# Two units through each TensorE array mode together: regrouping the stages of a chunked retention and mixture-of-adapters kernel

## The chip, the cores and the metric

The kernel runs on one core of a Trainium2 chip. The time is device microseconds of one execution. The kernel before takes 194.24 us (median of three runs, 193.79 to 195.04). The profiled execution has a span of 191.0 us, and TensorE was granted 0.993 of its full clock over it.

## The reference

Two layers are computed, one after the other. For 8 sequences and 8 heads, with 576 positions and a head size of 64, the first is retention: attention without a softmax, with a decay that differs by head.

```python
scores = scale * np.matmul(q, k.transpose(0, 1, 3, 2))
gamma = 1.0 - 2.0 ** (-5.0 - np.arange(H, dtype=np.float32))
Dmat = np.where(rel >= 0, gamma[:, None, None] ** rel[None, :, :], 0.0)
ret = scores * Dmat[None, :, :, :]
return np.matmul(ret, v)
```

Its result, read as 4608 tokens of 512 values, goes through a mixture of 8 adapters of rank 16. For each token the two experts with the largest of the 8 logits `x @ w_gate` are taken, their logits pass a softmax over the two, and the output is `x` plus the weighted sum of `(x @ A[e]) @ B[e]`. Everything is in fp32 at the borders; the kernel keeps the second, small adapter product in fp16.

## The kernel before, in words

**Tiling.** The 576 positions are cut into four full chunks of 128 and a last one of 64. Sequences are taken in quads of four: one quad of one chunk is loaded by three DMAs (q, k and v). A full quad has two *units* of two sequences each; in the last chunk a unit takes four sequences of 64 positions. So units 0 to 15 are full (two units to a quad, two quads to a chunk) and units 16 and 17 make up the last chunk. A state `P` per unit position carries the decayed sum of k-times-v from chunk to chunk, which keeps the work linear in the number of chunks.

**Stages of a unit.** Each is a function that emits its instructions.

- T (line 268): TensorE transposes q and k, 16 matmuls each, into two PSUM banks each; ScalarE or VectorE copies them out (`qT`, `kT`).
- S (326): scores, in two halves of 16 matmuls, one per sequence. Each half fills two whole PSUM banks (`ps`), and VectorE multiplies each by the decay mask on its way to SBUF (`rt`).
- Q (304): the part of the output that comes from `P`, into the two banks `px`. U (374): the new state (`pu`, then `pn` on VectorE and `P` on GpSimd). R (402): scores times v, added into `px`; VectorE scales each bank out into `xT`.
- Z (484): adapter-down product and gate logits together (`pz`), then four kinds of small VectorE instructions on the logits. V (511): two sigmoids on ScalarE. W (524): VectorE picks the two experts and weights the adapter values (`zc`).
- B (449): transposes `xT` back to token rows, into the two banks `po`, which stay held. X (469): transposes `zc` (`pzt`, copied to `zT` by ScalarE). Y (549): adapter-up product added into `po`; four copies of a half bank take the result to `osb`, and DMAs write it.

**Array modes.** By the rows and columns of the array that its matmuls use, each stage is of one of four kinds: T, S and B use 64 rows by 128 columns (the profile's `64*128`), Q uses `64*64`, U and R `128*64`, and X, Z and Y `128*128`. In the last chunk S, Q and R are all `64*64`.

**Order.** The order is written out by hand. The helper `chain` (line 73) ties every instruction of TensorE, VectorE and ScalarE to the one emitted before it on the same engine, so that each engine runs exactly in the order in which the code calls the stages. Semaphores are added where data or buffers require them. In the steady loop (lines 673 to 694) one unit passes S, T of the next unit, B of the unit before, Q, U, R, and then X, Z and Y.

**PSUM.** The kernel hands out the eight banks itself, oldest free one first:

```python
def bank(shape, name, dtype=FP32):
    n = free.pop(0)
    x = pp.tile(shape, dtype, tag=f"bank{n}", name=name)
```

`done` puts a bank at the end of the list when the stage that reads it has been emitted. The next tile on that bank then waits, at its first matmul, until the reader of the old one has finished. So what counts is how many other banks are handed out in between.

**Other buffers.** q, k and v have three buffers each, so the load for the quad after next is issued at a quad's start. GpSimd scales k in place after its transpose (`scale_k`, line 255).

Of the kernel before, what the change touches and what calls it, by code (L numbers as in the profile page):

```python
# [10 lines left out]
FP32 = mybir.dt.float32  # L11
# [7 lines left out]
def kernel(  # L19
# [232 lines left out]
    def is_full(t):  # L252
        return units[t][0] < NFULL

    def scale_k(t):

        if not is_full(t):
            return
        kk = nat[units[t]][1]
        for b in range(2):  # L260
            gp.tensor_tensor(  # L261
                out=kk[:, b],
                in0=kk[:, b],
                in1=gv[:, 0].unsqueeze(2).broadcast_to((128, H, Dh)),
                op=ALU.mult,
            )

    def stage_T(t, names=("qT", "kT")):

        s = st.setdefault(t, {})  # L270
        for nm in names:
            src = nat[units[t]][0 if nm == "qT" else 1]
            dst = s[nm] = wk.tile([128, 2, HP, C], FP32, tag=nm, name=nm)
            ps = [bank([128, HP, 2, L], f"p{nm}") for _ in range(2)]
            for hp in range(HP):
                for b in range(2):
                    for g in range(2):
                        mm(
                            ps[g][:, hp, b, :],
                            lhsT=src[rows(g), b, 2 * hp : 2 * hp + 2, :],  # L280
                            rhs=id64[rows(g), :],
                            is_transpose=True,
                            start=True,
                            stop=True,
                        )
            for g in range(2):
                if is_full(t):
                    o = dst[:, :, :, rows(g)].rearrange("p b a i -> p a b i")
                else:
                    o = dst[:, g].rearrange("p a (b i) -> p a b i", b=2)  # L290
                if t == 0 and nm == "kT":
                    for b in range(2):
                        x = dst[:, b, :, rows(g)]
                        if g == 1:
                            vec("tensor_copy", out=x, in_=ps[g][:, :, b])
                        else:
                            act("copy", out=x, in_=ps[g][:, :, b])
                elif t < 2 and nm == "qT" or t < 3 and nm == "kT" and g == 1:
                    vec("tensor_copy", out=o, in_=ps[g])
                else:  # L300
                    act("copy", out=o, in_=ps[g])
            done(*ps)
# [99 lines left out]
    def stage_R(t):  # L402
        c, qd, sl = units[t]
        s = st[t]
        px, rt = s["px"], s["rt"]
        v32 = nat[units[t]][2]
        s["xT"] = []
        if is_full(t):
            for b in range(2):
                for hp in range(HP):  # L410
                    for ho in range(2):
                        h = 2 * hp + ho
                        mm(
                            px[b][rows(ho ^ b), hp, :],
                            lhsT=v32[:, b, h, :],
                            rhs=rt[(b, ho)][:, hp, :],
                            start=(c == 0 and hp == 0),
                            stop=True,
                            skip_group_check=True,
                        )  # L420
                xt = mo.tile([128, HP, C], FP32, tag="xT", name="xT", bufs=6)
                vec("tensor_tensor", out=xt, in0=px[b], in1=asc[b], op=ALU.mult)
                s["xT"].append(xt)
            done(*px)
            return
        for hp in range(HP):
            for y in range(2):
                for ho in range(2):
                    for x in range(2):
                        mm(  # L430
                            px[x][rows(ho ^ x), hp, rows(y)],
                            lhsT=v32[rows(x), y, 2 * hp + ho, :],
                            rhs=rt[ho][rows(x), hp, y, :],
                            start=False,
                            stop=True,
                            skip_group_check=True,
                        )
        for x in range(2):
            xt = mo.tile([128, HP, C], FP32, tag="xT", name="xT", bufs=6)
            vec("tensor_tensor",   # L440
                out=xt.rearrange("p a (y i) -> p a y i", y=2),
                in0=px[x].rearrange("p a (y i) -> p a y i", y=2),
                in1=asc[x][:, :, 0:L].unsqueeze(2).broadcast_to((128, HP, 2, L)),
                op=ALU.mult,
            )
            s["xT"].append(xt)
        done(*px)
# [76 lines left out]
    def stage_W(t, gs=BOTH):  # L524
        s = st[t]
        n = len(gs)
        if len(s[("route", gs)]) == 4:
            stage_V(t, gs)
        lg, m8, ns, pz, sg = s.pop(("route", gs))
        cm = mo.tile([128, n, E], FP32, tag=f"cm{n}", name="cm")  # L530
        zc = mo.tile([128, n, ER], FP16, tag=f"zc{n}", name="zc")
        for y in range(n):
            vec(
                "scalar_tensor_tensor",
                out=cm[:, y, :], in0=pz[:, y, ER : ER + E], scalar=m8[:, y, 1:2], in1=sg[:, y, :],
                op0=ALU.is_ge, op1=ALU.mult,
            )
        for y, g in enumerate(gs):
            vec(
                "tensor_tensor",  # L540
                out=zc[:, y, :].rearrange("p (e r) -> p e r", e=E),
                in0=pz[:, y, 0:ER].rearrange("p (e r) -> p e r", e=E),
                in1=cm[:, y, :].unsqueeze(2).broadcast_to((128, E, R)),
                op=ALU.mult,
            )
            s.setdefault("zc", {})[g] = zc[:, y, :]
        done(pz)
# [65 lines left out]
    for t in range(NU):  # L613
        if units[t][2] == 0:
            issue(quads.index(units[t][:2]) + 2)
        if t == 0:
# [13 lines left out]
            stage_Q(0)  # L630
            stage_R(0)
            stage_T(1, ("qT",))
            stage_T(1, ("kT",))
            scale_k(1)
            stage_Z(0)
            stage_S(1)
# [5 lines left out]
            stage_B(0)  # L642
            stage_X(0)
            stage_Z(1)
            stage_Y(0, spread=True)
            stage_T(2, ("kT",))
            scale_k(2)
            for ho in range(2):
                gp.tensor_tensor(
                    out=maskh[ho], in0=trih.unsqueeze(1).broadcast_to((128, HP, L)),  # L650
                    in1=heads(1, ho, L), op=ALU.mult,
                )
            continue
        if t == 1:
            continue
        if t == NU - 1:
            break
        if t == 2:
            stage_T(3, ("qT",))
            stage_B(1)  # L660
            stage_V(1)
            stage_S(2)
            stage_W(1)
            stage_T(3, ("kT",))
            stage_U(2)
            stage_Q(2)
            scale_k(3)
            stage_R(2)
            stage_X(1)
            stage_Z(2)  # L670
            stage_Y(1)
            continue
        if is_full(t):
            stage_S(t, (0,))
            stage_V(t - 1)
            stage_T(t + 1, ("qT",))
            stage_S(t, (1,))
            stage_W(t - 1)
            stage_T(t + 1, ("kT",))
            stage_B(t - 1)  # L680
            if units[t][0] > 0:
                stage_Q(t)
            if not is_full(t + 1):
                stage_S(t + 1)
                stage_Q(t + 1)
            stage_U(t)
            scale_k(t + 1)
            if units[t][0] == 0:
                stage_Q(t)
            stage_R(t)  # L690
            stage_X(t - 1)
            stage_Z(t)
            stage_Y(t - 1)
            continue

        stage_W(t - 1)
        stage_T(t + 1)
        stage_B(t - 1)
        stage_R(t)
        stage_Q(t + 1)  # L700
        stage_X(t - 1)
        stage_Z(t)
        stage_W(t)
        stage_Y(t - 1)
        stage_S(t + 1)
        stage_B(t)
        stage_X(t)
        stage_R(t + 1)
        stage_Y(t)
        for g in range(2):  # L710
            stage_Z(t + 1, (g,))
            stage_W(t + 1, (g,))
        stage_B(t + 1)
        for g in range(2):
            stage_X(t + 1, (g,))
            stage_Y(t + 1, (g,), spread=True, last=True)
    return

# [1 line left out]
_INS = ['q', 'k', 'v', 'moe_w_gate', 'moe_A', 'moe_B']  # L720
_OUTS = [((4608, 512), 'float32')]
# [25 lines left out]
```

## Time and profile before

| What | Value |
|---|---|
| median of 3 runs | 194.24 us (193.79 to 195.04) |
| span of the profiled run | 191.0 us |
| TensorE matmuls, weight loads | 179.9 us busy (94%), 163.3 us (85%) |
| VectorE, ScalarE, GpSimd | 110.3, 72.1, 58.9 us busy |
| DMA, 20 to 140 us | 0.79 to 0.98 of the DMA engines' time, 231 to 263 GB/s |
| VectorE, multiply by mask, whole bank | 685 ns each, 64 of them |
| VectorE, `xT` out of `px`, whole bank | 690 ns each, 36 of them |
| ScalarE copy of `kT` or `qT`, whole bank | about 592 ns each, 64 of them |
| ScalarE copy of `osb`, half a bank | 385 ns each, 68 of them |

Busy time alone does not show what bounds a stage. A matmul's record overlaps that of the next, so that the pitch from one group's start to the next group's start is the group's price. In lines of a timeline the first column is the start in us, the second the time from the first start to the last end, then engine, operation, what is written and read, the shape, and the count. In brackets stands the idle time ahead of the group and what ended it.

### The profile page before, as it was taken

The page shows a single profiled execution, that of the slowest core. Times are in us where ns is not written, and L with a number is a line of the kernel's source. Part 1 is how long each engine was busy: PE and PEld are TensorE (multiplying, and loading weights), DVE is VectorE, ACT ScalarE, POOL GpSimd, SP SyncE. Part 2 cuts the span into 40 slices and gives each one's busy share as a digit, 9 for nine tenths or more (in the row PEclk, how much of TensorE's full clock was granted, in tenths as well). Part 3 has the DMA queues.
Part 4 walks back from the last instruction along what each step waited for, and adds up shares of the span by engine and source line. Part 5 has one row for each costly group of instructions (what it writes and reads, how often), then busy time and mean ns, then how long its engine had stood idle before and what let it go on. Part 6 is the DMA issues. An engine that isn't in the chain of part 4 may idle for free. (4 is left out here: it accounts for less than half of the span.)

```text
span 191.0 us, 8118 instructions
## 1 busy us (share of the span) xinstructions
PE 179.9 (94%) x3612; PEld 163.3 (85%) x3612; DVE 110.3 (58%) x282; ACT 72.1 (38%) x196; POOL 58.9 (31%) x70
## 2 busy tenths in 40 slices
PE   7899999999999999999999999999999998988870
PEld 2598999899999999999999999999999998977750
DVE  4476947484646474656564747565564646423650
ACT  4111163445344443526170707061625252070540
POOL 8994026040514242424242332415060600200000
PEclk9999999999999999999999999999999999999997
DMA  6999989896899699897879857989982020020343
GB/s 143 263 243 275 276 239 265 250 274 194 237 314 279 192 283 313 256 280 278 219 201 276 255 184 216 307 210 252 216 231 113 6 83 33 3 113 3 113 110 110
DMA packets 53746, 38.73 MB, mean 203 GB/s; under 512 B 27472, under 2 KB 49104, under 8 KB 53712
## 3 DMA queue, kind: packets, MB, share of 16 engines
q1 hardware_dynamic: 52736, 37.75, 70.3%
q8 instruction: 28, 0.46, 1.0%
q10 hardware_dynamic: 832, 0.34, 0.7%
q0 software_dynamic: 144, 0.13, 0.4%
q14 instruction: 6, 0.05, 0.1%
HBM read 28.91 MB, written 9.44 MB: 201 GB/s over the span
## 5 line engine op out<-in xcount | busy, mean ns | idle before, releaser
L261 POOL TENSOR_TENSOR k<-k,pack 128x512 f32<-128x512 f32 x32 | 32.7, 1043 | 78.6 <-PE pkT L81 73.3
L84 DVE TENSOR_TENSOR rt<-ps,mask 128x512 f32<-128x512 f32 x64 | 40.9, 685 | 16.2 <-PE ps L81 16.0
L81 PE MATMUL pz<-AW,xT 128*128 128x136 f32 x288 | 37.4, 283 | 0.2 <-DVE xT L84 0.2
L81 PE MATMUL ps<-qT,kT 64*128 64x128 f32 x512 | 35.7, 281 | 0.6 <-DVE kT L84 0.6
L81 PEld LDWEIGHTS pz<-AW,xT 128*128 128x128 f32 x288 | 34.6, 190 | 0.7 <-DVE xT L84 0.5
L81 PEld LDWEIGHTS ps<-qT,kT 64*128 64x128 f32 x512 | 31.0, 188 | 3.7 <-PE po L81 2.7
L87 ACT COPY osb<-po 128x256 f32<-128x256 f32 x68 | 20.6, 385 | 28.6 <-PE po L81 26.4
L81 PE MATMUL px<-rt,v 128*64 128x128 f32 x512 | 30.7, 273 | 0.0
L84 DVE TENSOR_TENSOR xT<-px,asc 128x512 f32<-128x512 f32 x36 | 24.6, 690 | 7.7 <-PE px L81 6.6
L81 PEld LDWEIGHTS px<-rt,v 128*64 128x64 f32 x512 | 27.7, 137 | 0.0
L87 ACT COPY zT<-pzt 128x256 f16<-128x256 f16 (+1 forms) x19 | 6.9, 361 | 52.7 <-PE pzt L81 52.7
L400 POOL TENSOR_TENSOR P<-pn,gdec 128x512 f32<-128x512 f32 x12 | 15.3, 1276 | 27.4 <-DVE pn L84 25.9
L87 ACT COPY kT<-pkT 128x512 f32<-128x512 f32 (+1 forms) x34 | 18.0, 580 | 14.1 <-PE pkT L81 14.0
L87 ACT COPY qT<-pqT 128x512 f32<-128x512 f32 x32 | 17.3, 593 | 8.1 <-PE pqT L81 8.1
L84 DVE COPY lg<-pz 128x16 f32<-128x16 f32 (+1 forms) x19 | 3.3, 173 | 26.8 <-PE pz L81 26.8
L81 PE MATMUL pu<-v,k 128*64 128x64 f32 x512 | 18.4, 225 | 0.0
L81 PEld LDWEIGHTS pu<-v,k 128*64 128x64 f32 x512 | 16.2, 138 | 2.3 <-issue 1.9
L81 PE MATMUL px<-qT,P 64*64 64x128 f32 (+1 forms) x512 | 16.1, 261 | 1.6 <-issue 1.6
L84 DVE TENSOR_TENSOR pn<-pu,P 128x512 f32<-128x512 f32 x12 | 8.3, 692 | 15.4 <-PE pu L81 15.4
L81 PEld LDWEIGHTS px<-qT,P 64*64 64x64 f32 x512 | 12.7, 133 | 2.7 <-issue 1.9
L81 PE MATMUL po<-id,xT 64*128 64x64 f32 x288 | 12.6, 224 | 1.1 <-DVE zc L84 1.1
L81 PE MATMUL pkT<-id,k 64*128 64x64 f32 x288 | 12.2, 223 | 0.3 <-DMA k<-in_k_dram 0.3
(51 smaller groups left out, 149.6 us busy)
## 6 DMA issues: line engine op xcount, KB each, us to landing
out_dram<-osb SPq DMA_DIRECT2D x32, 256.0 KB, 4.1
q<-in_q_dram SPq DMA_DIRECT2D x4, 512.0 KB, 6.5
k<-in_k_dram SPq DMA_DIRECT2D x4, 512.0 KB, 6.7
v<-in_v_dram SPq DMA_DIRECT2D x4, 512.0 KB, 7.1
out_dram<-osb SPq DMA_DIRECT2D x6, 128.0 KB, 2.3
Arow<-in_moe_A_dram SPq DMA_DIRECT2D x1, 256.0 KB, 5.1
out_dram<-osb ACTq DMA_DIRECT2D x2, 128.0 KB, 2.7
Bcat<-in_moe_B_dram POOLq DMA_DIRECT2D x1, 128.0 KB, 4.7
```

Source lines behind the costliest of these rows:

```text
L81: chain("pe", nc.tensor.matmul(*args, **kw))
L84: chain("dve", getattr(nc.vector, fn)(**kw))
L87: chain("act", getattr(nc.scalar, fn)(**kw))
L261: gp.tensor_tensor(out=kk[:, b], in0=kk[:, b], in1=gv[:, 0].unsqueeze(2).broadcast_to((128, H, Dh)), op=ALU.mult,)
L400: nc.gpsimd.tensor_tensor(out=Pt, in0=pn, in1=gdec, op=ALU.mult)
```

## The change

The loop now advances by a quad, and both units of the quad pass each array mode together. In quad `t` (its units are `t` and `t+1`) TensorE runs: T, S of both units and B of the two units of two quads back (all `64*128`); X and Y of those and Z of the two units of the quad before (`128*128`); Q of both units (`64*64`); U and R of both units (`128*64`). So there are four changes of mode to a quad in place of eight; the routing of a unit comes one quad after its retention and its output one quad later still. To make room, `xT` gets eight buffers and `zc` four. The flag `shared` lets VectorE take one of the two copies of a transpose for the first unit of a quad. The sigmoids (V) are emitted right after their Z. Quad 2 moves into the prologue, and in the last chunk the dense stages of units 16 and 17 alternate with adapter stages of older units.

```diff
-    def stage_T(t, names=("qT", "kT")):
+    def stage_T(t, names=("qT", "kT"), shared=False):
...
-                elif t < 2 and nm == "qT" or t < 3 and nm == "kT" and g == 1:
+                elif t < 2 and nm == "qT" or shared and g == 1:
                     vec("tensor_copy", out=o, in_=ps[g])
                 else:
                     act("copy", out=o, in_=ps[g])
...
-                xt = mo.tile([128, HP, C], FP32, tag="xT", name="xT", bufs=6)
+                xt = mo.tile([128, HP, C], FP32, tag="xT", name="xT", bufs=8)
...
-        zc = mo.tile([128, n, ER], FP16, tag=f"zc{n}", name="zc")
+        zc = mo.tile([128, n, ER], FP16, tag=f"zc{n}", name="zc", bufs=4)
...
             stage_Z(1)
+            stage_V(1)
             stage_Y(0, spread=True)
-            stage_T(2, ("kT",))
+            stage_T(2, ("kT",), shared=True)
+            stage_T(3)
             scale_k(2)
+            scale_k(3)
+            stage_S(2)
+            stage_W(1)
+            stage_S(3)
+            for u in (2, 3):
+                stage_U(u)
+                stage_Q(u)
+                stage_R(u)
...
-        if is_full(t):
-            stage_S(t, (0,))
-            stage_V(t - 1)
-            stage_T(t + 1, ("qT",))
-            stage_S(t, (1,))
-            stage_W(t - 1)
-            stage_T(t + 1, ("kT",))
-            stage_B(t - 1)
-            if units[t][0] > 0:
-                stage_Q(t)
-            if not is_full(t + 1):
-                stage_S(t + 1)
-                stage_Q(t + 1)
-            stage_U(t)
-            scale_k(t + 1)
...
-            stage_R(t)
-            stage_X(t - 1)
-            stage_Z(t)
-            stage_Y(t - 1)
-            continue
...
+        done_, near = [u for u in (t - 4, t - 3) if u > 0], (t - 2, t - 1)
+        here = (t, t + 1)
+        for nm in ("kT", "qT"):
+            stage_T(t, (nm,), shared=True)
+        scale_k(t)
+        for u in done_:
+            stage_B(u)
+        stage_T(t + 1, ("kT",))
+        scale_k(t + 1)
+        stage_S(t, (0,))
+        stage_T(t + 1, ("qT",))
+        stage_S(t, (1,))
+        stage_S(t + 1)
+        for u in done_:
+            stage_X(u)
+        stage_Z(near[0])
+        stage_V(near[0])
+        for u in done_:
+            stage_Y(u)
+        stage_Z(near[1])
+        stage_V(near[1])
+        if units[t][0] > 0:
+            for u in here:
+                stage_Q(u)
+        for u in near:
+            stage_W(u)
+        if t + 2 == NU - 2:
+            stage_T(t + 2)
+            stage_T(t + 3)
+        for u in here:
+            stage_U(u)
...
+            stage_R(u)
+
+    h, n = NU - 2, NU - 1
+    stage_S(h)
+    stage_Q(h)
+    stage_B(h - 4)
+    stage_B(h - 3)
+    stage_X(h - 4)
+    stage_X(h - 3)
+    stage_Z(h - 2)
+    stage_V(h - 2)
+    stage_Y(h - 4, spread=True)
+    stage_Y(h - 3, spread=True)
+    stage_W(h - 2)
+    stage_S(n)
+    stage_R(h)
+    stage_Z(h - 1)
+    stage_V(h - 1)
+    stage_Q(n)
+    stage_W(h - 1)
+    stage_B(h - 2)
+    stage_B(h - 1)
+    stage_X(h - 2)
+    stage_X(h - 1)
+    stage_Z(h)
+    stage_V(h)
+    stage_Y(h - 2, spread=True)
+    stage_Y(h - 1, spread=True)
+    stage_R(n)
+    stage_W(h)
+    stage_B(h)
+    stage_X(h)
+    for g in range(2):
+        stage_Z(n, (g,))
+        stage_W(n, (g,))
+    stage_Y(h)
+    stage_B(n)
+    for g in range(2):
+        stage_X(n, (g,))
+        stage_Y(n, (g,), spread=True, last=True)
```

More of the change, by code (lines that the diff above doesn't have):

```diff
@@ L438, in stage_R @@
         for x in range(2):
-            xt = mo.tile([128, HP, C], FP32, tag="xT", name="xT", bufs=6)
+            xt = mo.tile([128, HP, C], FP32, tag="xT", name="xT", bufs=8)
             vec("tensor_tensor",
@@ L632 @@
             stage_T(1, ("qT",))
-            stage_T(1, ("kT",))
+            stage_T(1, ("kT",), shared=True)
             scale_k(1)
@@ L653 @@
             continue
-        if t == 1:
+        if t < 4 or units[t][2] or not is_full(t):
             continue
[L656 to L671, printed above, removed]
-            continue
@@ L673 @@
-        if is_full(t):
-            stage_S(t, (0,))
-            stage_V(t - 1)
-            stage_T(t + 1, ("qT",))
-            stage_S(t, (1,))
-            stage_W(t - 1)
-            stage_T(t + 1, ("kT",))
-            stage_B(t - 1)
-            if units[t][0] > 0:
-                stage_Q(t)
-            if not is_full(t + 1):
-                stage_S(t + 1)
-                stage_Q(t + 1)
-            stage_U(t)
-            scale_k(t + 1)
-            if units[t][0] == 0:
-                stage_Q(t)
-            stage_R(t)
-            stage_X(t - 1)
-            stage_Z(t)
-            stage_Y(t - 1)
-            continue
@@ L696 @@
[L696 to L716, printed above, removed]
@@ L717 @@
-    return
+        done_, near = [u for u in (t - 4, t - 3) if u > 0], (t - 2, t - 1)
[14 more added lines that the diff above has]
+        stage_Z(near[0])
@@ new lines @@
+        stage_V(near[0])
[13 more added lines that the diff above has]
+            stage_U(u)
+            if units[t][0] == 0:
+                stage_Q(u)
+            stage_R(u)
+    h, n = NU - 2, NU - 1
```

## The prediction, on record before the result

> **What bounds the kernel now.** I read the page first: TensorE is busy without a break until the last chunk.
>
> ```profile
> PE 179.9 (94%) x3612; PEld 163.3 (85%) x3612; DVE 110.3 (58%) x282; ACT 72.1 (38%) x196; POOL 58.9 (31%) x70
> ...
> PE   7899999999999999999999999999999998988870
> ```
>
> Then the timeline of one steady unit, TensorE alone, for the price of each stage:
>
> ```profile
> 65.39 1.16 PE L81 MATMUL ps<-qT,kT 64*128 64x128 f32 x16
> 66.39 0.66 PE L81 MATMUL pqT<-id,q 64*128 64x64 f32 x16
> 66.88 1.11 PE L81 MATMUL ps<-qT,kT 64*128 64x128 f32 x16
> 67.83 0.65 PE L81 MATMUL pkT<-id,k 64*128 64x64 f32 x16
> 68.32 0.67 PE L81 MATMUL po<-id,xT 64*128 64x64 f32 x16
> 68.92 1.10 PE L81 MATMUL px<-qT,P 64*64 64x128 f32 x32
> 69.95 1.15 PE L81 MATMUL pu<-v,k 128*64 128x64 f32 x32
> 70.93 1.92 PE L81 MATMUL px<-rt,v 128*64 128x128 f32 x32
> 72.78 0.29 PE L81 MATMUL pzt<-ident,zc 128*128 128x128 f16 x2
> 72.91 2.07 PE L81 MATMUL pz<-AW,xT 128*128 128x136 f32 x16
> 74.81 0.60 PE L81 MATMUL po<-Bcat,zT 128*128 128x256 f16 x4
> 75.34 1.16 PE L81 MATMUL ps<-qT,kT 64*128 64x128 f32 x16
> ```
>
> No group carries an idle time: a unit takes 75.34 - 65.39 = 9.95 us and a quad 19.9, all TensorE. The starts give pitches: T 0.49 for either half, S 0.95 a half, B 0.49 without its switch (0.60 with), Q 1.03, U 0.98, R 1.85, X 0.13, Z 1.90, Y 0.53. A group's results are ready about 0.16 after the next group's start (66.39 against 65.39 + 1.16). The readers on the other engines, from the same stretch:
>
> ```profile
> 66.58 1.29 DVE L84 TENSOR_TENSOR rt<-ps,mask 128x512 f32<-128x512 f32 x2 [0.88 <-PE ps L81]
> 68.03 1.29 DVE L84 TENSOR_TENSOR rt<-ps,mask 128x512 f32<-128x512 f32 x2 [0.16 <-PE ps L81]
> ```
> ```profile
> 68.57 1.07 ACT L87 COPY kT<-pkT 128x512 f32<-128x512 f32 x2 [0.36 <-PE pkT L81]
> ```
>
> Half an S (0.95 us of TensorE) costs VectorE 1.29 us. In the tail of the old kernel one bank wait can be seen whole:
>
> ```profile
> 169.24 0.27 PE L81 MATMUL po<-id,xT 64*128 64x64 f32 x1
> ...
> 169.74 0.48 DVE L84 TENSOR_TENSOR zc<-pz,cm 128x128 f16<-128x128 f32 x2
> ...
> 170.37 0.68 PE L81 MATMUL po<-id,xT 64*128 64x64 f32 x15 [0.86 <-DVE zc L84]
> ```
>
> B's first matmul has its bank; the second needs the bank that held `pz` and stops until `zc` has read it. So bank order, not data, can stop TensorE.
>
> **What the Trainium skill says.** "TensorEngine Tiling (Array Packing)", Key Properties: changing the tiling mode drains the engine. The trace agrees: B takes 0.60 ahead of Q and T 0.49 with the same matmuls, so 0.11; the first S after Y takes 1.00 and the second 0.95. The same page, PSUM Bottleneck: tiling speeds up TensorE, not the emptying of PSUM, which may then bind; that is 0.95 against 1.29 here. "TensorE: Matmul & The Clock Gate", Architectural detail: VectorE and ScalarE are strictly first in, first out, and Part 3, The mechanism: matmuls keep their order. The tail above agrees: 15 matmuls stood behind one.
>
> **The change part by part.**
>
> *Removed: mode switches.* Bounds from the rows: 0.10 (drain alone) to 0.16 (0.11 + 0.05 of refill); I take 0.13. Four fewer to a quad: 0.52 us, so 19.9 becomes 19.4 if nothing waits. Over six quads about 3 us.
>
> *Added: bank waits.* B is now ahead of S and holds four banks until Y. I follow the list. All eight are free at a quad's start; T(t) takes a,b (k) and c,d (q) and gives them back; B takes the other four. From there until Y only a, b, c, d go round: T k(t+1) a,b; S(t) first half c,d; T q(t+1) a,b; S(t) second half c,d; S(t+1) a,b and c,d; X a, X b; Z c. Each must wait for the reader of the one two steps before. In the kernel before only `pz` was held there, and seven banks went round.
>
> The clock of a steady quad, 0 at T k(t), a release reaching TensorE 0.06 after the reader ends (estimated from 170.22 to 170.30 above):
> - T k, T q, both B, T k(t+1): 0 to 2.48. No waits: VectorE is free from 0.81, after the last `xT`, and has its two shared copies (682 ns, the row of `qT` on VectorE) done by 2.1.
> - S(t) first half 2.48 to 3.43. ScalarE copies kT(t+1) from 2.73 to 3.80. T q(t+1) could start at 3.43, gets a, waits for b until 3.86: **0.40 lost**, ends 4.33.
> - `rt` 3.62 to 4.91. S(t) second half gets c at 4.37, waits for d until 4.97: **0.60 lost**, ends 5.88.
> - S(t+1) first half: a,b free (qT copied 5.65); 5.88 to 6.83. `rt` of the half before 6.07 to 7.36. S(t+1) second half waits for d until 7.42: **0.53 lost**, ends 8.32, and 8.42 after the switch.
> - Remaining `rt` 7.27 to 8.56 and 8.51 to 9.80. X waits for b until 8.62 (**0.07**), ends 8.75; Z needs c at 9.26: **0.51 lost**, Z to 11.16.
> - Y, Y to 12.02; Z to 14.02. ScalarE, in order: `sg` of the first unit 12.05 to 12.57 (behind `lg`, `max`, `ns` on VectorE), eight `osb` copies, 0.28 apart, to 14.9, `sg` of the second to 15.4. Q(t) starts 14.02, Q(t+1) 14.98: its banks come from the first `po`, free at 13.84. W ends 16.25, ahead of `pn` at 17.1. No loss.
> - U, R, U, R: 15.95 to 21.5.
>
> Sum of the losses 2.1, less 0.5: **21.5 us a quad, against 19.9**.
>
> *Moved: the prologue.* Up to T k(2) at 26.73 the order is as before. Then T(3), S(2) (0.5 for ScalarE's copies behind two `sg` and two `osb`), S(3) (0.16), U and R twice: it ends at 38.5. Before, the same stages plus 7.0 us of others had ended at S(4), 45.5 (154.97 less 11 x 9.95). No gain. Loads: T q(4) had its data without waiting at 37.55, and GpSimd needs 2.04 per unit for k, so neither binds.
>
> *First quad.* Unit 0 is already out, so B holds two banks and six go round. Work 19.4 less 1.0 for B, X, Y of one unit, plus 0.9 for copies of q: 19.3, to 57.8. Quads 6 to 12: 4 x 21.5 = 86, to 143.8.
>
> *Quad 14* adds T(16) and T(17): 1.96, one switch 0.13, and waits for ScalarE's copies, four pairs of 1.07 against 0.98 of TensorE each: 0.88 + 0.48. So 25.1, to 168.9.
>
> *Last chunk.* Up to Z(17) TensorE has S 2.0, Q 2.0, B 2.45, X 0.65, Z(14 to 16) 5.7, Y 1.7, R 2.0 and a dozen switches, about 18.0 in all. Waits: Z(14) and Z(16) on the bank of X (0.65 each: a `pzt` just made has to be copied); S(17) on `po`, which ScalarE copies only after `sg` of 14 (1.1); X(16) on `zc`, queued on VectorE behind four `osb` copies of 0.42 and two `xT` behind R(17) (1.8). Less the parts that fall on switches: 21.6, to 190.5. From Z(17) to the end the old kernel took 191.0 - 181.31 = 9.7; now Y(16)'s four ScalarE copies (1.2) stand ahead of the last `zT`: 11.0. End 201.5, 10.5 more than 191.0: **194.24 + 10.5 = 204.7**.
>
> `xT`, `zc` and more buffers: nothing; their readers are a quad away. `shared` removes two copies from ScalarE a quad, which is why S(t) doesn't wait.
>
> **The rivals.**
> 1. *The bank waits don't appear* (readers faster than rows of before, or a pitch already slowed by them). For it: TensorE is the bound, and every switch removed is time won; the old tail also has holes (0.80, 0.86, 0.84 and smaller, about 3.5) that the new order fills. Against it: the wait at 169.24 and 1.29 against 0.95. Time: 3.0 for switches and about 4 from the tail: 187.
> 2. *Half of the waits*: some of the 2.1 a quad overlaps the drain, or the tail is filled. Five quads at +0.5 instead of +1.6, tail waits 2 less: 197.
> 3. *More waits than I found*: a wait on a semaphore that also covers a later reader, for instance T q stopping at b's and a's both; 0.5 more a quad and 1.5 in the tail: 209.
>
> **How the numbers follow.** Forecast 0.65, rival 1 0.08, rival 2 0.15, rival 3 0.12. The waits are built from measured rows and a bank order that the code fixes; the tail, of about 32 us, is the least certain, by 2 us, and the switch price by 0.03 x 25 = 0.8. Range 197 to 208.5: rival 1 is left out, with the outer part of rival 3. Faster 0.08, slower 0.87, same 0.05.
>
> **What would show it.** TensorE's share of its span near 85% and idle ahead of `pqT` on ScalarE's `kT`, of `ps` on VectorE's `rt` (about 1.1 a quad), of `pz` on `rt`; a period of 21.5 from one quad's first `pkT` to the next; 685 ns for `rt` unchanged; stages inside U, R and Z at the same pitch. The step that fails if I am wrong: that only four banks go round between B and Y, or the prices 1.29 and 1.07 that hold them.

## The result, and the profile after

The changed kernel takes 205.44 us (median of four runs, 204.13 to 206.29) against 194.11 us before: 1.057 times as long, with a 95% interval of 1.049 to 1.065. Forecast were 204.7 us and a range of 197 to 208.5. The profiled span went from 191.0 to 202.9 us. Here and below a median is of all runs, and a ratio leaves out runs over 1.5% longer than the fastest of their kernel.

The page's busy times and TensorE's row of slices, of the changed kernel:

```profile
PE 184.1 (91%) x3612; PEld 166.9 (82%) x3612; DVE 119.0 (59%) x302; ACT 62.3 (31%) x176; POOL 58.8 (29%) x70
...
PE   7897999999999999999898999999999989899750
```

The same 3612 matmuls are busy for longer (184.1 against 179.9 us), and yet their share fell. A matmul that stops for its bank after the group's first has been issued is still counted as busy for part of that time, so the losses are better read from the starts of groups. TensorE's timeline of the quad with units 8 and 9, behind the start of the quad before it (columns as before):

```profile
58.03 0.71 PE L81 MATMUL pkT<-id,k 64*128 64x64 f32 x16
...
79.56 0.71 PE L81 MATMUL pkT<-id,k 64*128 64x64 f32 x16
80.10 0.67 PE L81 MATMUL pqT<-id,q 64*128 64x64 f32 x16
80.61 1.16 PE L81 MATMUL po<-id,xT 64*128 64x64 f32 x32
81.61 0.67 PE L81 MATMUL pkT<-id,k 64*128 64x64 f32 x16
82.11 1.11 PE L81 MATMUL ps<-qT,kT 64*128 64x128 f32 x16
83.06 0.22 PE L81 MATMUL pqT<-id,q 64*128 64x64 f32 x1
83.49 0.71 PE L81 MATMUL pqT<-id,q 64*128 64x64 f32 x15 [0.22 <-ACT kT L87]
84.00 4.08 PE L81 MATMUL ps<-qT,kT 64*128 64x128 f32 x48
88.02 0.40 PE L81 MATMUL pzt<-ident,zc 128*128 128x128 f16 x4
88.72 2.12 PE L81 MATMUL pz<-AW,xT 128*128 128x136 f32 x16 [0.31 <-DVE rt L84]
...
100.13 0.39 PE L81 MATMUL pu<-v,k 128*64 128x64 f32 x6 [1.01 <-issue]
100.30 1.97 PE L81 MATMUL px<-rt,v 128*64 128x128 f32 x32
102.20 0.71 PE L81 MATMUL pkT<-id,k 64*128 64x64 f32 x16
```

The signature of a bank wait is `x1` and then `x15`: the first matmul has its bank, the second stops from 83.09 to 83.49. The three halves of S that follow take 88.02 - 84.00 = 4.02 us where three times 0.95 would be 2.85; about 0.1 of the difference is the change of mode behind them. Z starts 0.47 after X should have let it (X of two units took 0.23 in kernels where nothing stops it). The idle column shows only 0.22 and 0.31 of this; the pitch shows all.

ScalarE and VectorE in the same stretch have the readers that were awaited, no slower than before:

```profile
82.36 1.07 ACT L87 COPY kT<-pkT 128x512 f32<-128x512 f32 x2 [0.91 <-PE pkT L81]
```
```profile
83.25 1.29 DVE L84 TENSOR_TENSOR rt<-ps,mask 128x512 f32<-128x512 f32 x2 [1.63 <-PE ps L81]
85.58 3.68 DVE L84 TENSOR_TENSOR rt<-ps,mask 128x512 f32<-128x512 f32 x6 [1.04 <-PE ps L81]
```

ScalarE's copy of k ends at 83.43, and the transposes of q go on at 83.49. VectorE waits for TensorE (1.04 us) and TensorE for VectorE, in turn: two stages that hand the same two banks back and forth. From the waits, the weight loads (PEld) that stopped longest in steady quads:

```profile
PEld ps L81 <- DVE rt L84: 3.0, 10, 0.3
PEld pz L81 <- DVE rt L84: 2.4, 5, 0.5
...
PEld pqT L81 <- ACT kT L87: 1.8, 5, 0.4
```

Ten waits of S and five of Z for `rt`, five of q's transpose for `kT`: twice, once and once in each of quads 6 to 14. The first `pkT` of quads 6, 8 and 14 (named by their first unit) start at 58.03, 79.56 and 145.10 us, of quad 4 at 39.14, and the last chunk at 170.16. Quads 6, 8, 10 and 12 take 21.53, 22.64, 21.40 and 21.50 us. The one shown is the longest, by a stop of 1.01 us in a U for which the profile shows no wait ("issue"); such stops come back in the experiments and are no part of the bank waits.

### The profile page after: what moved, and what is told of

The parts are those of the page before. It is cut to its first block, busy times and chain, and to the rows that moved or that the text cites. A ratio compares the mean times of both kernels' runs of the same rounds, so it can differ in the third digit from the quotient of the medians.

```text
span 202.9 us, 8133 instructions
## 1 busy us (share of the span) xinstructions
PE 184.1 (91%) x3612; PEld 166.9 (82%) x3612; DVE 119.0 (59%) x302; ACT 62.3 (31%) x176; POOL 58.8 (29%) x70
## 5 line engine op out<-in xcount | busy, mean ns | idle before, releaser
L84 DVE TENSOR_TENSOR rt<-ps,mask 128x512 f32<-128x512 f32 x64 | 39.8, 683 | 18.0 <-PE ps L81 17.8
L81 PE MATMUL ps<-qT,kT 64*128 64x128 f32 x512 | 37.3, 282 | 2.0 <-DVE kT L84 0.6
L261 POOL TENSOR_TENSOR k<-k,pack 128x512 f32<-128x512 f32 x32 | 32.5, 1042 | 21.4 <-PE pkT L81 20.4
L81 PEld LDWEIGHTS ps<-qT,kT 64*128 64x128 f32 x512 | 32.7, 188 | 4.5 <-DVE rt L84 3.0
L87 ACT COPY kT<-pkT 128x512 f32<-128x512 f32 (+1 forms) x28 | 15.1, 579 | 58.5 <-PE pkT L81 50.1
L87 ACT ACTIVATE sg<-lg,ns 128x8 f32<-128x8 f32 x36 | 9.0, 294 | 32.2 <-DVE ns L84 31.8
L87 ACT COPY osb<-po 128x256 f32<-128x256 f32 x60 | 17.3, 386 | 1.0 <-PE po L81 0.6
L87 ACT COPY qT<-pqT 128x512 f32<-128x512 f32 x26 | 14.3, 590 | 10.4 <-PE pqT L81 10.3
L81 PE MATMUL pqT<-id,q 64*128 64x64 f32 x288 | 13.9, 227 | 1.5 <-ACT kT L87 1.1
L81 PE MATMUL pkT<-id,k 64*128 64x64 f32 x288 | 13.2, 227 | 1.5 <-DMA k<-in_k_dram 1.2
L81 PE MATMUL px<-qT,P 64*64 64x128 f32 (+1 forms) x512 | 14.3, 260 | 0.0
```

The costliest lines, as they stand in the source:

```text
L81: chain("pe", nc.tensor.matmul(*args, **kw))
L84: chain("dve", getattr(nc.vector, fn)(**kw))
L87: chain("act", getattr(nc.scalar, fn)(**kw))
L261: gp.tensor_tensor(out=kk[:, b], in0=kk[:, b], in1=gv[:, 0].unsqueeze(2).broadcast_to((128, H, Dh)), op=ALU.mult,)
```

## The experiments

Each ratio is to the kernel before, measured on the same chip in the same rounds.

**1. B behind S.** In the changed kernel, so that eight banks go round during T and S:

```diff
-        for u in done_:
-            stage_B(u)
         stage_T(t + 1, ("kT",))
...
         stage_S(t + 1)
+        for u in done_:
+            stage_B(u)
```

> The changed kernel with B of both older units moved from ahead of S to behind it (still in the same array mode), so that all eight banks go round during T and S in place of four. Bank theory: S no longer waits for the bank of the half before; what is left is data (S waits 0.66 us for the copy of q of the first unit, since no B fills that time, and 0.43 for the copy of q of the second), so a quad takes 19.4 + 1.1 = 20.5 us in place of 21.5, and the kernel about 200.5 us. Rival, VectorE's rate alone (eight rt of 0.60 us against 3.8 us of S) stops TensorE whatever the banks: no change, 205. Rival, passing both units through a mode together costs in itself: no change, 205.

Measured: 199.47 us, ratio 1.027 (1.022 to 1.032). A steady quad:

```profile
83.03 0.71 PE L81 MATMUL pkT<-id,k 64*128 64x64 f32 x16
83.57 0.67 PE L81 MATMUL pqT<-id,q 64*128 64x64 f32 x16
84.08 0.67 PE L81 MATMUL pkT<-id,k 64*128 64x64 f32 x16
85.24 1.16 PE L81 MATMUL ps<-qT,kT 64*128 64x128 f32 x16 [0.49 <-DVE qT L84]
86.20 0.69 PE L81 MATMUL pqT<-id,q 64*128 64x64 f32 x16
86.70 1.14 PE L81 MATMUL ps<-qT,kT 64*128 64x128 f32 x16
88.08 2.06 PE L81 MATMUL ps<-qT,kT 64*128 64x128 f32 x32 [0.23 <-ACT qT L87]
89.97 1.16 PE L81 MATMUL po<-id,xT 64*128 64x64 f32 x32
...
103.46 0.71 PE L81 MATMUL pkT<-id,k 64*128 64x64 f32 x16
```

The quad takes 103.46 - 83.03 = 20.43 us (20.5 expected). No transpose is split any more, and two halves of S in a row take 1.89 us. VectorE does the same eight `rt` and now needs 5.35 us from the first to the last, for 6.01 in the changed kernel's quad, so its rate did not set the stop; how many banks stood between S and it did. The two waits left are for data, as expected: 0.67 and 0.43 us by the starts. (This profile begins with a wait of 3.0 us for a load, so its span is not used here.)

**2. More mode changes in the old kernel**, by moving B to between U and R:

```diff
             stage_T(t + 1, ("kT",))
-            stage_B(t - 1)
...
             if units[t][0] == 0:
                 stage_Q(t)
+            stage_B(t - 1)
             stage_R(t)
```

> The kernel before with B moved to between U and R, which adds two changes of array mode to each of 13 units and nothing else; banks are free by then. With 0.13 us for a change: 26 x 0.13 = 3.4 us more, about 197.5 us. With 0.10 it is 196.7, with 0.16 198.3. If a change of mode costs nothing that is not hidden, 194; if it costs twice what I took, 201.

Measured: 197.70 us, ratio 1.020 (1.016 to 1.025); 3.5 us over the 194.17 of its rounds, 0.14 for each of 26 changes. TensorE around the moved stage:

```profile
77.22 1.16 PE L81 MATMUL ps<-qT,kT 64*128 64x128 f32 x16
...
81.28 1.15 PE L81 MATMUL pu<-v,k 128*64 128x64 f32 x32
82.36 0.71 PE L81 MATMUL po<-id,xT 64*128 64x64 f32 x16
83.01 1.97 PE L81 MATMUL px<-rt,v 128*64 128x128 f32 x32
...
87.47 1.16 PE L81 MATMUL ps<-qT,kT 64*128 64x128 f32 x16
```

A unit takes 10.25 us in place of 9.95: 0.15 a change. B takes 0.65 between two other modes and 0.49 beside its own. So the gain that the change was after is real.

**3 and 4. Fewer banks in the old kernel**, nothing regrouped: two banks, or one, are withheld for units 3 to 14.

```diff
+        if t == 3:
+            kept = [free.pop() for _ in range(2)]
+        if t == 15:
+            free.extend(kept)
```

> The kernel before with two of the eight banks withheld for units 3 to 14, the order of all work unchanged. Bank theory, by the same clock as in the prediction: per unit the second half of S waits 0.40 for rt, B 0.42 for the second half's rt, Q 0.65 for zc, together 1.47 us; twelve units make 17.6, so about 212 us, with TensorE's waits naming rt and zc. Rival, VectorE's rate: it is busy 5.9 of 9.95 us a unit here and its work is unchanged, so 194. Rival, the regrouping costs in itself: 194.

> The kernel before with one of the eight banks withheld for units 3 to 14. Bank theory: Q waits 0.40 for the second half's rt and T of k 0.07, so 0.47 per unit and 5.6 in all, about 199.8 us. Rivals: 194.

Measured with two fewer: 209.96 us, ratio 1.082 (1.075 to 1.089). With one fewer: 199.33 us, ratio 1.028 (1.023 to 1.033). The waits of the kernel with two fewer:

```profile
PEld px L81 <- DVE zc L84: 4.7, 11, 0.4
...
PEld po L81 <- DVE rt L84: 2.6, 12, 0.2
...
PEld ps L81 <- DVE rt L84: 2.4, 12, 0.2
```

These are the three waits that the clock of banks named, about once a unit each. The starts of one group in two units that follow each other, first with two fewer, then with one fewer:

```profile
86.16 1.10 PE L81 MATMUL px<-qT,P 64*64 64x128 f32 x30 [0.19 <-DVE zc L84]
...
97.51 1.10 PE L81 MATMUL px<-qT,P 64*64 64x128 f32 x30 [0.19 <-DVE zc L84]
```
```profile
88.46 1.16 PE L81 MATMUL ps<-qT,kT 64*128 64x128 f32 x16
...
98.86 1.16 PE L81 MATMUL ps<-qT,kT 64*128 64x128 f32 x16
```

A unit takes 11.35 us with two fewer, 1.40 more than before where 1.47 was worked out, and 10.40 with one fewer, 0.45 more where 0.47 was. With one fewer the view of waits names no reader in the steady units; the starts put 0.30 of the 0.45 in Q and 0.10 in T of k, where the clock of banks had it. The old order, left as it was, loses time in the same way as the new one when banks are taken from it. Both rivals, VectorE's rate and a cost of regrouping, said 194.

**5. W of unit 16 first in VectorE's queue**, in the changed kernel's last chunk:

```diff
     stage_V(h)
-    stage_Y(h - 2, spread=True)
-    stage_Y(h - 1, spread=True)
+    stage_W(h)
+    stage_Y(h - 2)
+    stage_Y(h - 1)
     stage_R(n)
-    stage_W(h)
     stage_B(h)
```

> The changed kernel, in the last chunk only: W of unit 16 goes ahead of the output copies of units 14 and 15 on VectorE, and ScalarE makes all eight of these copies. If X(16) waits for zc because of VectorE's queue (four copies of 0.42 and two xT ahead of it), Z(17) starts about 1.6 us earlier and the kernel takes about 203.9 us. Rival, the end is set elsewhere (ScalarE's queue ahead of the last zT, which now gets longer): no change, 205.4.

Measured: 203.75 us, ratio 1.045 (1.036 to 1.054), an interval that overlaps the changed kernel's (1.049 to 1.065), so the profiles have to say what was gained. This wait of X(16), stage X of unit 16, in the changed kernel is gone:

```profile
191.19 0.43 PE L81 MATMUL pzt<-ident,zc 128*128 128x128 f16 x2 [1.25 <-DVE zc L84]
```

From the last chunk's start to Z(17) it takes 20.0 us (170.96 to 190.97) in place of 21.3, and to the end 31.4 in place of 32.7. The 1.3 us are what that queue cost.

**6. Another order for the last chunk**, the loop as changed:

```diff
     stage_Q(h)
     stage_B(h - 4)
-    stage_B(h - 3)
     stage_X(h - 4)
     stage_X(h - 3)
     stage_Z(h - 2)
...
     stage_Y(h - 4, spread=True)
-    stage_Y(h - 3, spread=True)
+    stage_Z(h - 1)
+    stage_V(h - 1)
     stage_W(h - 2)
     stage_S(n)
     stage_R(h)
-    stage_Z(h - 1)
-    stage_V(h - 1)
     stage_Q(n)
     stage_W(h - 1)
+    stage_B(h - 3)
     stage_B(h - 2)
...
```

What is left out moves Y(13) behind X(15), B(15) and Y(15) behind R(17), W(16) ahead of R(17) and X(16) behind Z(17), and lets VectorE share the output copies of unit 16.

> The changed kernel with its loop as it is and another order for the last chunk: B of unit 13 a step later, so that Z never needs the bank of an X just made, output copies of 12 to 16 shared by both engines, W of 16 ahead of R of 17. If the tail's excess over its 17 us of TensorE work is those waits, Z(17) starts about 4 us earlier and the kernel takes about 201 us. Rival, the tail is set by the chain of routing of single units: under 1 us gained, 204.5.

Measured: 201.13 us, ratio 1.035 (1.027 to 1.044), about as expected, but for reasons that agree only in part. By the profile Z(17) starts 18.8 us after the last chunk does (168.38 to 187.18) in place of 21.3: 2.5 gained and not 4; a new stop of 1.25 us ("issue") within Q(17) is most of the difference. From the last chunk's start to the end it takes 30.4 us in place of 32.7. The rest of the 4.1 us between the two profiles lies ahead of the last chunk, where both run the same program: the changed kernel's has 0.8 us more of waits for k's load at the start and the stop of 1.0 us in one U, 1.8 us in all. So by the profiles the tail itself is worth some 2.3 us, with the new stop in it.

**7 and 8. Transposes a quad ahead**, with the changed tail, and with the tail of experiment 6:

```diff
...
+        slots = [(t, 0), (t, 1), (t + 1, 0), (t + 1, 1)]
+        ahead = [(t + 2, "qT"), (t + 2, "kT"), (t + 3, "qT"), (t + 3, "kT")]
+        for (u, b), (v_, nm) in zip(slots, ahead):
+            stage_S(u, (b,))
+            stage_T(v_, (nm,))
+            if nm == "kT":
+                scale_k(v_)
         for u in done_:
             stage_B(u)
...
```

> The changed kernel with both transposes made one quad ahead: each of the four halves of S is followed by one T of the next quad, B of both older units comes behind them, four buffers for qT and kT; the tail as changed. Each half of S now has 0.49 us of other work behind it (1.44 us to VectorE's 1.29) and all eight banks go round. Bank theory: no waits in the quad, 19.4 us a quad in place of 21.5, and 1.4 us of waits of T(16) and T(17) gone; four quads at -2.1, quad 14 at -5.6 and the first at +1.5 make about -13, so about 192.4 us. Rival, VectorE's rate or the regrouping itself: 21 us a quad or more, over 202.

> Both: transposes a quad ahead and the other order of the last chunk. If the two losses are separate they add up: -13 and -4 from 205.4, about 188.4 us, faster than the kernel before. Rival, the tail's waits come back because the loop leaves other banks: 192.

Measured: 202.21 us, ratio 1.037 (1.029 to 1.046), and 200.66 us, ratio 1.033 (1.025 to 1.040). They missed by ten and twelve us. The first reached its rival's number (over 202), but not for the rival's reason, as its waits say:

```profile
PE pqT L81 <- DMA q<-in_q_dram: 8.8, 1, 8.8
```

Quad 4 now transposes quad 6's q at about 42 us, and its load lands at 50.7; k and the second unit follow slowly, so that S(4) to S(5) take from 40.73 to 59.15. From 46 to 58 us TensorE's granted clock was 0.50, and half an S took 1.81 us (55.19 to 57.00). So this first quad takes 33.6 us (38.51 to 72.08) where the changed kernel's takes 18.9. From the next quad on, the theory's number holds: 72.08 to 91.38 us is 19.30 for a quad. Neither the regrouping nor VectorE's rate is in the way; the loads of the first four quads are.

**9. Transposes ahead from quad 8 on**, when the loads have got ahead; quad 6 has B behind S.

```diff
+        if t < 8:
+            for nm in ("kT", "qT"):
+                stage_T(t, (nm,), shared=True)
...
+        else:
+            if t == 8:
+                for u in here:
+                    for nm in ("qT", "kT"):
+                        stage_T(u, (nm,), shared=True)
+                    scale_k(u)
```

> Transposes a quad ahead only from quad 8 on, when loads have got ahead of the work; quad 4 as in the changed kernel, quad 6 with B behind S; the tail as changed. If the whole miss of the first try was the third quad's load, quads 10 to 14 take 19.3 us each, quad 6 20.4, quad 8 about 21.4 (its own transposes come first), so the last chunk starts near 157.7 instead of 170.2: about 193 us. Rival, the loads pace the kernel for longer: TensorE waits for q or k again in quads 8 to 10, 197 or more.

Measured: 192.43 us (19 runs), ratio 0.990 (0.987 to 0.994). A steady quad's first part:

```profile
99.31 1.16 PE L81 MATMUL ps<-qT,kT 64*128 64x128 f32 x16
100.30 0.66 PE L81 MATMUL pqT<-id,q 64*128 64x64 f32 x16
100.80 1.11 PE L81 MATMUL ps<-qT,kT 64*128 64x128 f32 x16
101.75 0.66 PE L81 MATMUL pkT<-id,k 64*128 64x64 f32 x16
102.24 1.12 PE L81 MATMUL ps<-qT,kT 64*128 64x128 f32 x16
...
118.61 1.16 PE L81 MATMUL ps<-qT,kT 64*128 64x128 f32 x16
```

S, T, S, T at the old pitches, no idle, 19.30 us a quad, and the last chunk starts at 157.2 us (157.7 expected). The regrouping, with its bank waits removed, is faster than the kernel before by 0.6 us a quad. The last chunk is still the changed kernel's here, so the loop alone gave back the whole loss, from a ratio of 1.057 to 0.990.

**10. Both**, experiment 9's loop and experiment 6's last chunk, and in that X(16) ahead of Z(17) again:

```diff
     stage_B(h)
+    stage_X(h)
     stage_Y(h - 1, spread=True)
```

> The same with the other order of the last chunk, and in it X of unit 16 ahead of Z of 17, so that ScalarE's zT is not queued behind the sigmoids. If the losses of loop and tail are separate, 4.3 less for the tail as measured and up to 1.6 less for this wait: 187.5 to 189 us, faster than the kernel before by 2.5 to 3.5%. Rival: the tail gives back half, 191.

Measured: 190.58 us, ratio 0.980 (0.973 to 0.987). The tail gave 1.9 us more, not 4 to 6, and the rival (191, half given back) was the nearer: by the profiles of experiment 6 the order was worth 2.3 on its own, and this profile again has a stop within Q(17), of 1.50 us:

```profile
165.51 1.16 PE L81 MATMUL pe<-qT,kT 64*64 64x64 f32 x64
166.50 1.11 PE L81 MATMUL px<-rh,v 64*64 64x64 f32 x64
167.43 0.88 PE L81 MATMUL px<-qT,P 64*64 64x64 f32 x47
169.82 0.47 PE L81 MATMUL px<-qT,P 64*64 64x64 f32 x17 [1.50 <-issue]
```

"issue" means that no wait explains it.

**11. Z(15) moved into that stretch**, against the kernel of experiment 10:

```diff
-    stage_Z(h - 1)
-    stage_V(h - 1)
     stage_W(h - 2)
     stage_S(n)
     stage_R(h)
+    stage_Z(h - 1)
+    stage_V(h - 1)
     stage_Q(n)
```

> The last kernel lost 1.50 us inside Q of unit 17, while TensorE waited for nothing that the profile shows, after 175 small matmuls in a row (S of 17, R of 16, Q of 17, at about 15 ns each). Here Z of unit 15 stands between R of 16 and Q of 17, at the price of two more changes of array mode (0.3 us). If the stop comes from a long dense stretch of small matmuls, it goes: about 189.4 us. If it is bound to Q itself or comes by chance, it stays or moves: 190.9.

Measured: 188.70 us, ratio 0.972 (0.965 to 0.979), the lowest here, though the interval overlaps experiment 10's. Its profile has no such stop, and the last chunk takes 29.2 us from its start to the end in place of 30.4:

```profile
162.31 1.16 PE L81 MATMUL pe<-qT,kT 64*64 64x64 f32 x64
163.29 1.11 PE L81 MATMUL px<-rh,v 64*64 64x64 f32 x64
164.33 2.12 PE L81 MATMUL pz<-AW,xT 128*128 128x136 f32 x16
166.38 1.16 PE L81 MATMUL px<-qT,P 64*64 64x64 f32 x64
```

## Why the prediction was right, step by step

- **Mode changes** were slightly undersized. 0.13 us was taken from a span of 0.10 to 0.16; experiment 2 gives 0.14 to 0.15, and a quad free of waits takes 19.30, so four changes are worth 0.60 and not 0.52. "TensorEngine Tiling (Array Packing)" of the Trainium skill, Key Properties, says that a change of mode drains the engine; here it has a price.
- **Four banks go round between B and Y**: shown, from two sides. Giving the banks back (experiment 1) takes a quad from 21.5 to 20.4; taking banks from the old order (3 and 4) brings the waits there. The predicted clock holds to about 0.1 us at every step: 0.40 lost in T q(t+1) (0.40 measured), 4.09 from the second half of S to X, with the change of mode (4.02), 0.5 ahead of Z (0.47). The quads without a stop took 21.40 to 21.53 us where 21.5 was worked out, and waits cost them 21.5 - 19.3 = 2.2 us. One of the clock's inputs was a poor reading that came out well: the release of 0.06 us leans on a start at 170.30 that no line has (the line shown has 170.37, and `zc` ends at 170.22). In the changed kernel the copy's end and the next transpose, 83.43 and 83.49, do lie 0.06 apart.
- **The prologue** ended at 39.14 us and not 38.5; this profile waited 1.2 us for loads of k, and experiment 9's, which waited 0.2, has 38.50. No gain there, as forecast. **The first quad** took 18.9 for 19.3. **Quad 14** took 25.06 for 25.1, though the terms given for it add up to 24.95.
- **The last chunk** was right in sum: Z(17) 21.3 us after its start for 21.6, and 11.45 to the end for 11.0. Some of this is luck. Each of its four waits came out smaller than worked out (0.5 twice for 0.65, 0.9 for 1.1, 1.3 for 1.8), and the 0.6 that the sum took off for parts that fall on changes of mode made up for most of that. Two of its terms were tested: the queue ahead of `zc` was worth 1.3 us by the profile, and the order as a whole 2.3. The wait of `po` for the last `zT` behind four copies is in the trace (1.46 us).
- **The total** ended 1.4 us later than worked out, 202.9 for 201.5 in the profile: 0.6 from the prologue, 0.4 less in the first quad, 1.0 from the stop in quad 8, and 0.1 in the last chunk. The stop and the longer load wait were not in the prediction.
- **Rival 1**, no bank waits, said 187 and was wrong about this order; a tuned order of the same idea, with another last chunk, ends at 188.7. **Rivals 2 and 3** would need a quad of about 20.4 or 22.0 us; the quads without a stop took 21.40 to 21.53.
- **A sign that failed**: TensorE's share was to be near 85% and is 91%, because stopped matmuls count as busy in part. That step used the wrong view; the pitch would have been the one to name.

Not settled by any run is the stop without a shown wait, but the traces say more of it than the views do. Thirteen profiles hold fifteen of them, nine in Q of the last chunk and six in U, S or R. Counted from the start, with the semaphore instructions among them, TensorE's instructions (matmuls and weight loads are one each) put every stop at the same place in blocks of 256: behind 1985, 3521 to 3523, 3777, 6337 or 6849 to 6851 instructions, always 193 to 195 over a multiple of 256. The page lists 28 packets of kind "instruction" with 0.46 MB, so 16 KB each, and TensorE's 7290 or so instructions make 28.5 such blocks. Every stop ended 1.2 to 1.6 us after one of these packets had ended. So the stops look like TensorE waiting for its next block of instructions. In a stretch where matmuls follow at 15 ns, 128 of them with their weight loads, a whole block, pass in 2 us. That fits experiment 11, where Z's slower matmuls stand in the stretch and the stop is gone; it is a reading of the traces, and no run took the instructions' supply itself as its variable.

## What to carry to other kernels

When stages are regrouped, count how many other banks are handed out between two uses of the same one, and compare the work in that gap with the reader's time: half an S of 0.95 us and a transpose of 0.49 cover a reader of 1.29 us, and half an S alone does not. A stage that holds banks for long (B until Y) belongs behind the stages that need them in rotation, and short stages of the same array mode belong between the long ones. A prefetch that moves work a stage earlier must be checked against the landing of the first loads too: experiment 7 won 2.2 us in each later quad, and its first took 33.6 us in place of 18.9.

## What the runs showed of the hardware

- A change of array mode cost TensorE 0.14 to 0.15 us, from 26 added changes and from the unit's period.
- During the wait of 8.8 us for a load TensorE's granted clock fell: 1.00 until 44 us, 0.50 from 46 to 58, and half an S took 1.81 us in place of 0.95 there. "TensorE: Matmul & The Clock Gate", Part 1, says that an idle TensorE loses half its clock until it has been busy again; the trace agrees.
- A matmul that waited for a bank went on 0.06 us after the reader's end (83.43 to 83.49, and 148.98 to 149.04 in the changed kernel).
- Stops of TensorE of 0.3 to 1.5 us with no wait shown came in nine of thirteen profiles, each 193 to 195 instructions over a multiple of 256 and 1.2 to 1.6 us after a 16 KB packet of instructions had ended.
